# Turning the fourth plain group by blocks on VectorE, with two changes of the weave, in an attention + Fourier-mix + MLP kernel

## Chip, cores, metric

One core of one Trainium2 chip. The metric is the device time of one execution in microseconds, as the median of several runs. A profile's own span is some 1.8 us shorter than the time of its run.

## The reference

Linear attention with decay over blocks, for batch 4, 8 heads, 768 positions, head size 64; then a Fourier mix of the 4 x 768 x 512 result, a layer norm, and an MLP with 2048 hidden units. All in float32.

```python
# attention, per block of 64 positions
intra = einsum('bhic,bhjc->bhij', qb, kb) * Dmask
out   = einsum('bhij,bhjd->bhid', intra, vb) + einsum('bhid,bhde->bhie', qb * lam_pow, kv_state)
kv_state = lam_block * kv_state + einsum('bhsd,bhse->bhde', kb * rev_pow, vb)
# mix and MLP on x = (4, 768, 512)
u  = x + real(fft(fft(x, axis=1), axis=2))
un = (u - mean(u)) / sqrt(var(u) + 1e-06)
y  = u + maximum(un @ w_ch1, 0) @ w_ch2          # 512 -> 2048 -> 512
```

## The kernel before: the parts that matter

A **front** is one batch's attention and Fourier mix. The mixed rows form 12 groups of 256 rows (4 batches x 3). The first four groups in order are **plain**: their MLP products are woven into the fronts of the later batches, so that TensorE has something to do while a front waits. The other eight are done at the end by a scheme with combined weights (the **late** stage). An MLP product needs the normalised rows transposed. Plain groups are turned on TensorE; late ones by 32x32 blocks on VectorE, and four DMAs per tile put the blocks in place in DRAM:

```python
plain = (b, g) in PLAIN                      # PLAIN = the first four of (b, g)
if plain:
    ut = uts[b, g] = new(up, [128, KO, G * 128], "ut")            # 3 buffers
else:
    to = utd[b, g] = dram.tile([128, KO, G * 128], F32, ...)
for i in range(G):
    un = new(np_, [128, DM], "un", bufs=1)
    # ... two tensor_scalar per tile: (x - mean) * rsqrt
    if plain:
        pt = psum_a([128, KO, 128])                               # a whole PSUM bank
        for c in range(KO):
            mm = nc.tensor.transpose(pt[:, c, :], un[:, 128 * c:128 * c + 128], ident)
            # ... (cut)
        nc.scalar.copy(ut[:, :, 128 * i:128 * i + 128], pt)
    else:
        uq = new(ep, [128, DM], "e")                              # ep has 2 buffers
        nc.vector.transpose(uq, un)
        for r in range(0, 128, 32):
            # ... (cut: dst, src)
            nc.sync.dma_start(dst, src)
    yield 0.7
```

The same two `e` buffers serve the unpacking of the float64 weights, which goes on until 227 us:

```python
e = ep.tile([128, 2 * WP], U16, tag="e", ...)
nc.sync.dma_start(raw, src.bitcast(U32))
nc.scalar.activation(sg, top.bitcast(I16), AF.Sign)               # L216, writes e
# ... L217 to L225: VectorE and ScalarE make one float32 piece of w from raw and e
```

and the loads of each attention chunk are issued by SyncE, like the block stores and the weight loads:

```python
for t, src in ((kt, k), (qt, q), (vt, v)):
    nc.sync.dma_start(t, src[b, :, rows, :].rearrange("h p d -> p h d"))
```

Every `yield` of a generator says how much nominal work it has just handed out; a weave takes plain work by the side of front work in a fixed ratio. The program's order is then rearranged once, when the kernel is built, by a scheduler that knows buffers and estimated times. In the traces here each engine works off its list in the order so fixed.

## Time and profile before

| | before |
|---|---|
| time, median of the first 3 runs (and of 6) | 823.18 us (822.48 us) |
| first plain product; first late product | 96.2 us; 428.1 us |
| TensorE idle, 96.2 to 428.3 us | 6.5 us |
| TensorE busy, share of the span | 97% |
| VectorE, ScalarE busy | 53%, 23% |

The stage to look at lies between the first plain and the first late product. TensorE is the bound there, so what counts is its idle time in that stage and what each piece of it waited for. In the profile lines PE is TensorE, PEld its weight loads, DVE VectorE, ACT ScalarE, POOL GpSimd and SPq SyncE's DMA issues; L332 is line 332 of the kernel; `sc<-pa` means that `sc` is written from `pa`, and `A <- B` that A waited for B.

### The profile page before, as it was taken

How to read it: one execution, taken by the hardware profiler on the slowest of the kernel's cores; microseconds unless marked ns; L12 is line 12 of the kernel's file. 1: busy time of each engine (PE TensorE's matmuls, PEld its weight loads, DVE VectorE, ACT ScalarE, POOL GpSimd, SP SyncE). 2: the span in 40 equal slices, each digit the busy share in tenths (PEclk: the TensorE clock that was granted, in tenths of full speed). 3: DMA queues.
4: the chain of work that ended last, by engine and by line, in shares of the span. 5: the costliest groups of instructions: out<-in, count | busy, mean ns of one | idle time of the engine just before them, and what ended most of it. 6: DMA issues, size and time to landing. Idle time of an engine off the chain costs nothing.

```text
span 819.4 us, 11694 instructions
## 1 busy us (share of the span) xinstructions
PE 795.2 (97%) x4608; PEld 634.9 (77%) x4608; DVE 437.8 (53%) x1018; ACT 186.5 (23%) x448; POOL 86.1 (11%) x102
## 2 busy tenths in 40 slices
PE   6989899999999999999999999999999999999998
PEld 5777767768585857768648888888888888888886
DVE  5899798766743761354895541165313661146311
ACT  3756344225420211312002200022001210022100
POOL 3223340011011010220000000000000000000000
PEclk9999999999999999999999999999999999999999
DMA  9979624248741136530351011100111001010010
GB/s 233 249 154 271 174 90 129 63 113 201 203 125 51 52 62 131 129 123 26 93 162 42 1 53 51 52 1 1 64 40 52 0 1 39 33 33 0 1 39 26
DMA packets 126684, 68.88 MB, mean 84 GB/s; under 512 B 111150, under 2 KB 112174, under 8 KB 126630
## 3 DMA queue, kind: packets, MB, share of 16 engines
q1 hardware_dynamic: 121488, 55.67, 26.6%
q0 software_dynamic: 2112, 6.69, 2.4%
q10 hardware_dynamic: 3030, 5.78, 1.9%
q8 instruction: 36, 0.59, 0.3%
q14 instruction: 18, 0.15, 0.1%
HBM read 48.72 MB, written 19.40 MB: 83 GB/s over the span
## 4 chain that ended last, share of the span: by engine, by line
PE 80%; DVE 10%; issue 4%; DMA 3%; ACT 2%; POOL 1%; POOLq 0%; ACTq 0%; DVEq 0%
PE p L770 24%; PE p L723 24%; PE pm L650 10%; PE pm L636 8%; PE pa L332 3%; PE pa L516 3%; PE pa L298 3%; DMA x<-xb,ix 2%; PE pa L328 2%; PE pa L274 1%; DVE sc L302 1%; PE pa L315 1%; PE pa L348 1%; PE pa L279 1%; DVE stt L546 1%
## 5 line engine op out<-in xcount | busy, mean ns | idle before, releaser
L636 PE MATMUL pm<-ut,w 128*128 128x256 f32 x512 | 119.2, 382 | 0.0
L650 PE MATMUL pm<-w,hr 128*128 128x512 f32 x256 | 115.8, 597 | 0.2 <-DVE w L225 0.2
L636 PEld LDWEIGHTS pm<-ut,w 128*128 128x128 f32 x512 | 94.4, 190 | 15.4 <-issue 3.6
L723 PE MATMUL p<-ur,w 128*128 128x256 f32 x384 | 93.8, 379 | 0.0
L650 PEld LDWEIGHTS pm<-w,hr 128*128 128x128 f32 x256 | 46.6, 190 | 49.5 <-issue 48.0
L723 PEld LDWEIGHTS p<-ur,w 128*128 128x128 f32 x384 | 73.0, 190 | 10.3 <-issue 0.5
L723 PE MATMUL p<-us,w1s 128*128 128x256 f32 x256 | 65.7, 379 | 0.0
L770 PE MATMUL p<-w,hs 128*128 128x256 f32 x256 | 58.0, 379 | 0.5 <-DVE y L791 0.5
L770 PE MATMUL p<-w2s,hs 128*128 128x256 f32 x256 | 57.9, 379 | 0.0
L770 PE MATMUL p<-w,ha 128*128 128x256 f32 x256 | 57.9, 379 | 0.0
L770 PEld LDWEIGHTS p<-w,hs 128*128 128x128 f32 x256 | 48.5, 190 | 7.5 <-DVE y L791 0.9
L625 POOL DMA_INDIRECT out_dram<-y,ix x12 | 11.9, 989 | 402.6 <-DVE y L796 342.6
L770 PEld LDWEIGHTS p<-w2s,hs 128*128 128x128 f32 x256 | 48.6, 190 | 6.6
L723 PEld LDWEIGHTS p<-us,w1s 128*128 128x128 f32 x256 | 48.6, 190 | 6.6
L770 PEld LDWEIGHTS p<-w,ha 128*128 128x128 f32 x256 | 48.6, 190 | 6.6
L750 ACT COPY ha<-p 128x256 f32<-128x256 f32 x32 | 11.9, 372 | 169.1 <-PE p L723 139.4
L761 DVE TENSOR_TENSOR ha<-p,ha 128x256 f32<-128x256 f32 x32 | 13.6, 424 | 45.2 <-ACT ha L760 45.2
L298 PEld LDWEIGHTS pa<-qT,kT 64*128 64x128 f32 x384 | 26.0, 193 | 13.2 <-ACT qT L281 7.3
L302 DVE TENSOR_TENSOR sc<-pa,decay 128x512 f32<-128x512 f32 x48 | 31.5, 683 | 8.8 <-PE pa L298 8.5
L332 PE MATMUL pa<-sc,v 128*64 128x128 f32 x384 | 32.1, 284 | 4.1 <-DVE sc L302 4.1
L298 PE MATMUL pa<-qT,kT 64*128 64x128 f32 x384 | 30.7, 292 | 3.2 <-ACT qT L281 2.9
L270 POOL TENSOR_TENSOR kd<-k,decay 128x512 f32<-128x512 f32 x20 | 23.0, 1152 | 94.8 <-PE pa L315 64.5
(144 smaller groups left out, 1135.0 us busy)
## 6 DMA issues: line engine op xcount, KB each, us to landing
raw<-in_moe_w_ch_dram SPq DMA_DIRECT2D x32, 512.0 KB, 4.8
k<-in_k_dram SPq DMA_DIRECT2D x24, 256.0 KB, 5.0
q<-in_q_dram SPq DMA_DIRECT2D x24, 256.0 KB, 5.9
v<-in_v_dram SPq DMA_DIRECT2D x24, 256.0 KB, 4.9
ud<-x SPq DMA_DIRECT2D x16, 256.0 KB, 2.3
utd<-e SPq DMA_DIRECT2D x64, 64.0 KB, 2.2
u<-ud SPq DMA_DIRECT2D x16, 256.0 KB, 2.7
ur<-utd SPq DMA_DIRECT2D x6, 512.0 KB, 4.3
```

The lines of the kernel that those rows point to most:

```text
L270: nc.gpsimd.tensor_tensor(kd, kt, kpow, op=ALU.mult)
L298: mm(pss[hi][:, hp, :], lhsT=kT[HD[hi], hp, :], rhs=qT[HD[hi], hp, :], start=True, stop=True)
L302: nc.vector.tensor_tensor(t, pss[hi], decay[:, hi::2, :], op=ALU.mult)
L328: mm(po[HD[hi], hp, :], lhsT=s_old[HD[hi], hp, :], rhs=qs[HD[hi], hp, :], start=(hp == 0), stop=False, skip_group_check=True)
L332: mm(po[HD[hi], hp, :], lhsT=vt[:, 2 * hp + hi, :], rhs=sc[hi][:, hp, :], start=(c == 0 and hp == 0), stop=(hp == HP - 1), skip_group_chec ...
L516: mm = nc.tensor.matmul(ps[0:m, n, :], lhsT=piece(a, i, n), rhs=cs[0:rows, a, i in (2, 3), n, :], start=(a == 0), stop=(a == 1))
L625: nc.gpsimd.indirect_dma_start(out=out.rearrange("b s d -> (b s) d"), out_offset=row_of(2 + HC * (b + 1) + T - HC), in_=y[:, :], in_offset ...
L636: nc.tensor.matmul(ps, lhsT=w1[:, c, 128 * fc:128 * fc + 128], rhs=ut[:, c, :], start=(c == 0), stop=(c == KO - 1))
L650: nc.tensor.matmul(ps, lhsT=hr[(fc - f0) // 4][:, fc % 4, 128 * i:128 * i + 128], rhs=w2[:, fc, :], start=(fc == f0), stop=(fc == f1 - 1))
L723: nc.tensor.matmul(ps, lhsT=s2.A[a][:, kt, 128 * i:128 * i + 128], rhs=U[b][:, kt, :], start=(first and kt == 0), stop=(kt == 1), skip_gro ...
L761: V.tensor_tensor(a22, two(Z), a22, op=ADD)
L770: nc.tensor.matmul(ps, lhsT=h[a][:, s, i, :], rhs=s2.B[b][:, i, :], start=(first and i == 0), stop=(i == HF - 1), skip_group_check=True)
```

## The change

The intent: take eight transposes, with the wait ahead of them and two parked PSUM banks, off TensorE for the fourth plain group by turning it on VectorE; put more plain work where the last batch's first chunk waits for its masked scores; and keep some more plain work for the handover to the late stage.

```diff
-        yield 1.5
+        yield 3.0 if (b, c) == (B - 1, 0) else 1.5
...
-                    mm(pu[HD[hi], hp, :], lhsT=kd[:, h, :], rhs=vt[:, h, :], start=True, stop=True)
+                    i = mm(pu[HD[hi], hp, :], lhsT=kd[:, h, :], rhs=vt[:, h, :], start=True, stop=True)
+                    if (b, c, h) == (B - 1, 0, 0):
+                        tc.keep_in_program_order(i)
...
-            plain = (b, g) in PLAIN
-            if plain:
+            plain, turned = (b, g) in PLAIN, (b, g) in PLAIN[:3]
+            if turned:
...
+    def fetch(n):
+        ut = uts[PLAIN[n]] = new(up, [128, KO, G * 128], "ut")
+        nc.sync.dma_start(ut, utd[PLAIN[n]])
...
+        if f0 > 0 and (b, g) == PLAIN[1]:
+            fetch(3)
...
-    t_rest, t_back = 3 * t_front - 5 * t_chunk, len(PLAIN) * t_mlp - 50.0
+    t_rest, t_back = 3 * t_front - 5 * t_chunk, len(PLAIN) * t_mlp - 54.0
```

(The second `if plain:` became `if turned:` too.)

More of the change, by code (lines that the diff above doesn't have):

```diff
@@ L565, in norm @@
                                             op0=ALU.subtract, op1=ALU.mult)
-                if plain:
+                if turned:
                     pt = psum_a([128, KO, 128])
```

## The prediction

> **What bounds the kernel now.** I read the stretches first: one table with busy times for the loading stage (0 to 96 us), the mixed stage in which fronts (attention and Fourier mix) and plain products (the MLP of four groups, lines L636 and L650) share TensorE (96 to 404), the handover (404 to 428.5) and the late stage of combined products.
>
> ```profile
> core 0: us, PE busy (x) PEld busy (x) DVE busy (x) ACT busy (x) POOL busy (x), PEclk, DMA share, GB/s
> 0.00:96.00 96.00, 82.31 (x930) 67.15 (x931) 80.73 (x167) 53.03 (x117) 30.47 (x38) 1.00 0.87 215
> 96.00:404.00 308.00, 301.54 (x1832) 216.97 (x1831) 189.73 (x432) 85.42 (x204) 46.86 (x55) 1.00 0.42 110
> 404.00:428.50 24.50, 24.50 (x59) 10.98 (x58) 24.41 (x30) 0.00 (x0) 0.02 (x1) 1.00 0.45 116
> 428.50:819.40 390.90, 386.84 (x1792) 339.84 (x1790) 142.88 (x391) 48.06 (x128) 8.76 (x9) 1.00 0.09 29
> ```
>
> TensorE is the bound from 96 us on, at full clock. In the mixed stage it is idle for 308.00 - 301.54 = 6.46 us; in the handover it is never idle, but VectorE is full too (24.41 of 24.50). The change is not in force before 96 us, and the late stage's work is untouched. So time can come only from those 6.46 us, or from TensorE work that goes away. The list of TensorE's waits in 96 to 428 says whose they are (total, times, longest):
>
> ```profile
> PE pa L569 <- DVE un L564: 2.6, 3, 1.0
> PE pa L516 <- DVE fe L475: 2.1, 3, 1.0
> PE pa L332 <- DVE sc L302: 1.6, 1, 1.6
> PE pm L650 <- DVE w L225: 0.2, 1, 0.2
> ```
>
> They add up to 6.5, so nothing is missing. L569 is the TensorE transpose of a normalised plain group; three of the four groups show a wait there in this stretch. L332 waits once, for the masked scores `sc`. The timeline of TensorE places both. First the turning of the fourth plain group, batch 1 group 1 (columns: start, duration, what, count, idle before and its releaser):
>
> ```profile
> 147.63 0.76 PE L569 MATMUL pa<-ident,un 128*128 128x128 f32 x4 [0.94 <-DVE un L564]
> 148.23 1.03 PE L636 MATMUL pm<-ut,w 128*128 128x256 f32 x4
> 149.10 0.60 PE L569 MATMUL pa<-ident,un 128*128 128x128 f32 x4
> 149.54 0.39 PE L529 MATMUL pa<-dt,ys 128*128 128x128 f32 x2
> ```
>
> then the last batch's first chunk:
>
> ```profile
> 290.70 1.45 PE L650 MATMUL pm<-w,hr 128*128 128x512 f32 x3
> 292.08 0.69 PE L315 MATMUL pa<-v,kd 128*64 128x64 f32 x16
> 294.35 0.43 PE L332 MATMUL pa<-sc,v 128*64 128x128 f32 x2 [1.59 <-DVE sc L302]
> ```
>
> Last, ScalarE's copies out of PSUM. The transposes of the fourth group end near 149.7, but its two copies run here, as one row of the timeline:
>
> ```profile
> 245.83 1.07 ACT L573 COPY ut<-pa 128x512 f32<-128x512 f32 x2 [1.34 <-PE pm L636]
> ```
>
> The `ut` pool has three buffers and this is the fourth group, so the copies wait until the first group's second half has read its buffer. Meanwhile two of the five `pa` banks of PSUM are held for about 245.8 - 149.7 = 96 us.
>
> **What the Trainium skill says.** "TensorE: Matmul & The Clock Gate", Part 4: PE-mode transpose: a full 128x128 transpose in one shot, but the output goes to PSUM and has to be copied out. The trace agrees: eight L569 matmuls and two 0.53 us copies for this group. "VectorE: DVE Perf Modes", The three transpose paths: VectorE turns 32x32 blocks only, not the whole tile. The trace agrees: each block-turned tile (L577, 128x512) is followed by four DMAs that put the blocks in place; one L577 takes 682 to 712 ns (median 700). "PSUM — Partial Sum Buffer", The four PSUM rules: a matmul output is at most one bank, 512 fp32 columns. `pt` is 512 columns, a whole bank, so the two parked tiles are two of the 5 + 3 banks that the pools hold.
>
> **Part 1, the fourth group turned by blocks.** Removed from TensorE: eight transposes. First four: the next matmul starts at 148.23, so 148.23 - 147.63 = 0.60 us of slot (they run in two bursts as the halves of `un` arrive). Second four: 149.54 - 149.10 = 0.44 us. Also the 0.94 us idle ahead of the first. L636 products follow these transposes at once and their `ut` is older, so I take it that TensorE goes on with them. Sum 0.60 + 0.44 + 0.94 = 1.98 us, all on the path, because TensorE is the bound at that point. Removed from ScalarE: two copies, 1.07 us, and an in-order wait of 1.34 us; ScalarE is busy 85 of 308 us here, so worth nothing by itself. Two `pa` banks come free, but no TensorE wait between 150 and 245 is in the list, so I count 0 for them.
>
> Added: two L577 of 0.70 us on VectorE at 148 to 150. There it waited anyway (0.53 us before the second `un` pair, 2.21 us before the L599 at 151.38), so 0 on the path. Added to the DMA queue of SyncE: eight 64 KB stores (median 2.2 us to landing) and one 512 KB fetch (the same transfer by `ur<-utd` took 4.3 us). The fetch can run once the first `ut` buffer is free, near 246 us. The group's first product comes about 362 (L636 has no instances between 326 and 362, where group three ends and four begins). Over 100 us of slack: 0 on the path.
>
> **Part 2, more plain products in the last batch's first chunk.** After the masked scores the front hands back 3.0 units in place of 1.5. The weave ratio is about 0.85, so 1.5 more units call for some 1.3 more units of plain work. This is granular: here the next item is an L650 step of four column blocks, 8 matmuls, and a run of 8 takes 3.4 to 3.6 us in the chain of waits. The pin keeps the state product L315 behind them. The stall is 1.59 us, so one step covers it: -1.6 us. It is the same product, done earlier, not more work.
>
> **Part 3, 54 units kept in place of 50.** The step of 3.4 units taken earlier would be missing at the handover, where VectorE's chain (combining weights, L700, then L713 to L716) ends at 427.88 + 0.68 = 428.56 us, and TensorE's plain products end at 428.3. There is no slack: had TensorE got there 3.6 us sooner with the fronts' end unmoved, it would wait. Four units more held back than before, less the 3.4 spent, bring the fronts' end forward by 0.6 us on top of what parts 1 and 2 save, so VectorE's chain ends earlier by about 3.6 + 0.6 = 4.2 us and TensorE's by 3.6. Own worth: 0, but it lets the other two arrive.
>
> **Sum.** -1.98 - 1.59 = -3.6 us; 823.18 - 3.6 = 819.6 us, ratio 0.9957.
>
> **Rivals.** (a) VectorE becomes the bound at the handover. For it: the last stretch is 24.41 of 24.50 us full on VectorE and both engines end within 0.3 us of each other. Against it: part 3, whose size matches. If it bites, 2 to 3.6 us come back: 821.5 to 823. (b) The interleaving shifts and makes other waits. Two L516 waits of about 1 us (258.9 to 260.0 and before 372.37) hang on VectorE's folding `fe` coming just too late; freed banks let batch 2's front run closer to its place, and the new weave ratio moves plain work around both. Either can vanish or double: -2 to +2 us. For it: all waits in the list are VectorE results arriving about 1 us late. Against it: the order of work within the fronts is unchanged. (c) The block path costs in the queue: the two turned tiles take both `e` buffers, which unpacking of weights (L216 at 151.22) also uses, until the stores land about 4 us later. In the list a late weight cost TensorE only 0.2 us, and the last weight is ready at 227 us, some 20 us before the products of the second half that read it; up to +1 us. (d) The fetch blocks the queue behind it: its landing slot falls where SyncE issues little (only `v` at 240.02 and `out_dram` at 253.48 between 234 and 254), so under 0.5 us. (e) Freed banks help more than I count, by fewer changes between attention and plain products: up to -1.5 us.
>
> **Range and chances.** The middle is -3.6. Rivals (a), (c) and (d) pull up, (b) is even, (e) pulls down. Runs of the kernel before spread over 821.59 to 825.39, so a median can be off by 1 us by itself. I take 819.6 with 816.8 to 822.8 for 8 in 10. Faster by over 2% would need 16.5 us, more than the whole idle time of the mixed stage: 1%. Slower by over 2% would need a new stall of 20 us net: 1%.
>
> **What would show it.** Right: L569 has 24 matmuls and not 32, L573 6 copies and not 8, L577 18 and not 16, 72 stores to `utd` and not 64; the wait of L569 falls from 2.6 to about 1.7 us; the 1.6 us of L332 is gone; TensorE's idle time between 96 us and the first late product falls from 6.5 to about 4, and the late stage starts near 424.7 us and lasts 391 us as before. Wrong: a new wait on `us` or `w1s` at the start of the late stage (rival a), larger waits on `fe` at L516 (b), TensorE waiting on `w` (c), L332 still waiting on `sc` (part 2's step did not come to lie there), or a time before 96 us that has moved, which nothing here explains.

## The result

826.95 us (825.71 to 828.04, 6 runs) against 822.48 us: ratio 1.0050, 95% interval 1.0031 to 1.0069. The change made the kernel slower by 0.5% where 0.4% faster was predicted; the time lies outside the predicted range. A ratio here is the mean time of one kernel's runs over that of the other's of the same rounds, so not quite the ratio of the medians quoted.

In the changed kernel the lines below the edits have moved: L332 is now L335, L516 L519, L569 L572, L577 L580, L581 L584, L636 L645, L644 L653, L650 L659.

The engines' instructions come in the same order in both kernels up to some 135 us, and the late stage lasts 391.3 and 391.2 us. The first plain product was at 96.2 and 97.1 us: that difference comes before the orders part, so it belongs to the two executions and not to the change (in the profiles of all runs it lies between 95.4 and 99.2 us). From the first plain to the first late product it took 331.9 us before and 335.7 us after. The loss lies there. Stretches of that stage, kernel before (columns: stretch, its length, then busy time and instructions of TensorE, weight loads, VectorE, ScalarE, GpSimd, clock, DMA share, GB/s):

```profile
96.20:155.00 58.80, 56.00 (x265) 41.69 (x264) 49.12 (x119) 22.94 (x56) 11.41 (x9) 1.00 0.33 107
155.00:210.00 55.00, 55.00 (x360) 37.02 (x359) 40.05 (x82) 21.59 (x45) 7.14 (x10) 1.00 0.65 162
```

and the changed kernel (one stretch more; before, it was 194.00 long with 190.34 us busy):

```profile
97.05:155.00 57.95, 56.03 (x265) 41.55 (x264) 50.04 (x122) 22.15 (x57) 11.66 (x9) 1.00 0.34 99
155.00:210.00 55.00, 48.66 (x343) 33.81 (x342) 36.79 (x77) 20.93 (x42) 7.54 (x10) 1.00 0.66 164
210.00:404.00 194.00, 189.93 (x1204) 137.22 (x1203) 102.10 (x234) 40.79 (x103) 27.59 (x34) 1.00 0.40 102
```

Length less TensorE's busy time is its idle time. In the first stretch it fell from 2.80 to 1.92 us: the wait ahead of the fourth group's transposes is gone, as predicted. In the second it rose **from 0 to 6.34 us**. This is where the time went, 10 to 45 us after the group was turned. The list of TensorE's waits in the changed kernel (96 to 433 us; total, times, longest) has three lines there that the list of before does not have:

```profile
PE pa L519 <- DVE fe L478: 2.8, 4, 1.0
PE pa L274 <- DMA k<-in_k_dram: 2.6, 1, 2.6
PE pm L645 <- ACT hr L653: 2.1, 1, 2.1
PE pa L572 <- DVE un L567: 1.7, 2, 1.0
PE pa L298 <- ACT qT L281: 1.5, 1, 1.5
PE pa L335 <- DVE sc L302: 1.4, 2, 1.3
PE pm L659 <- DVE w L225: 0.2, 1, 0.2
```

TensorE waits for a load (`k`), for a relu copy out of PSUM (`hr`) and for a copy (`qT`): 2.6 + 2.1 + 1.5 = 6.2 us. None of the three tiles belongs to the fourth group. Its own wait fell as forecast (L569's 2.6 us to L572's 1.7 us), and the wait for `sc` shrank by 0.2 us only.

**The late k load.** The timeline of SyncE's issues, kernel before (start, time from the first start to the last end of the merged issues, what, count):

```profile
172.44 5.27 SPq L581 DMA_DIRECT2D utd<-e  x8
...
181.24 0.38 SPq L263 DMA_DIRECT2D k<-in_k_dram  x1
```

and the changed kernel:

```profile
172.12 0.42 SPq L209 DMA_DIRECT2D raw<-in_moe_w_ch_dram  x1
182.36 5.70 SPq L584 DMA_DIRECT2D utd<-e  x8
...
189.29 0.38 SPq L263 DMA_DIRECT2D k<-in_k_dram  x1
```

In both, the k load of batch 2's third chunk stands behind the eight block stores of batch 1's last group. Those stores went out from 172.4 us before and from 182.4 us after; nothing at all is issued between 172.5 and 182.4. So the k load went out 8.05 us later. The next line is from TensorE's timeline of the changed kernel:

```profile
195.50 0.63 PE L274 MATMUL pa<-ident,k 128*128 128x128 f32 x4 [2.57 <-DMA k<-in_k_dram]
```

Why were the stores late? Batch 1 now has three block-turned groups, six tiles, in place of two groups. They pass through the two `e` buffers, alternately with the weight unpacking. The order in which VectorE does all this was fixed when the kernel was built. VectorE's timeline of the changed kernel:

```profile
173.70 0.69 DVE L285 TENSOR_TENSOR qs<-pa,qpow 128x512 f32<-128x512 f32 x1 [5.37 <-ACT qT L281]
...
180.96 0.42 DVE L217 TENSOR_SCALAR e<-raw 128x512 uint16<-128x512 uint16 x1
...
181.63 0.70 DVE L580 STREAM_TRANSPOSE e<-un 128x512 f32<-128x512 f32 x1
```

The last group's first block transpose (L580) stands behind a chunk of attention and a piece of weight unpacking (L217), and while its turn has not come VectorE idles 5.37 us for `qT`.

**The late relu copies.** ScalarE's timeline of the changed kernel:

```profile
182.59 0.58 ACT L338 COPY oT<-pa 128x512 f32<-128x512 f32 x1 [0.46 <-PE pa L335]
186.75 0.66 ACT L216 ACTIVATE e<-raw 128x512 bf16<-128x512 int16 x1 [3.57 <-DMA utd<-e]
...
187.92 0.91 ACT L653 ACTIVATE hr<-pm 128x256 f32<-128x256 f32 x3
```

The weight unpacking L216 needs an `e` buffer and waits 3.57 us for the landing of a block store that still reads it. Three relu copies stand behind it in ScalarE's order, so three product banks of PSUM stay full and TensorE waits 2.1 us. The `qT` wait at 161.5 us comes through the same list, though no buffer is waited for there: the copies of kT and qT stand behind an L218 that had waited 3.92 us for VectorE's L217, and L217 stood behind norm work in VectorE's order.

**The sc wait.** The extra plain step came where it should: eight L659 matmuls from 293.5 us, between the state product and L335. But VectorE does the two halves of the masked scores apart:

```profile
295.68 0.65 DVE L302 TENSOR_TENSOR sc<-pa,decay 128x512 f32<-128x512 f32 x1
296.25 0.69 DVE L580 STREAM_TRANSPOSE e<-un 128x512 f32<-128x512 f32 x1
...
298.17 0.65 DVE L302 TENSOR_TENSOR sc<-pa,decay 128x512 f32<-128x512 f32 x1
```

In the kernel before they follow each other (two L302 in 1.28 us from 293.62). Now 1.9 us of batch 2's block transpose and norm (L580, L549, L567, L550) come between, so the step covers the wait for the first half and TensorE waits 1.27 us for the second. The 1.59 us of before were for the first half alone: L332 began at 294.35, right after it, and the second was ready when TensorE came to it.

### The profile page after: what moved, and what is told of

Same layout as the page of the kernel before. It is cut to its first block, busy times and chain, and to the rows that moved or that the text cites. A ratio compares the mean times of both kernels' runs of the same rounds, so it can differ in the third digit from the quotient of the medians.

```text
span 823.9 us, 11693 instructions
## 1 busy us (share of the span) xinstructions
PE 792.8 (96%) x4600; PEld 633.3 (77%) x4600; DVE 437.2 (53%) x1020; ACT 184.9 (22%) x446; POOL 86.7 (11%) x102
## 4 chain that ended last, share of the span: by engine, by line
PE 77%; DVE 12%; DMA 4%; issue 4%; ACT 2%; POOL 1%; SPq 0%; DVEq 0%; POOLq 0%; ACTq 0%
PE p L779 24%; PE p L732 23%; PE pm L659 9%; PE pm L645 7%; PE pa L335 3%; PE pa L519 3%; PE pa L298 2%; DMA x<-xb,ix 2%; PE pa L331 1%; DMA raw<-in_moe_w_ch_dram 1%; DVE sc L302 1%; PE pa L316 1%; DVE w L224 1%; PE pa L274 1%; DVE stt L549 1%
## 5 line engine op out<-in xcount | busy, mean ns | idle before, releaser
L645 PE MATMUL pm<-ut,w 128*128 128x256 f32 x512 | 119.2, 382 | 2.1 <-ACT hr L653 2.1
L659 PE MATMUL pm<-w,hr 128*128 128x512 f32 x256 | 115.2, 596 | 0.2 <-DVE w L225 0.2
L645 PEld LDWEIGHTS pm<-ut,w 128*128 128x128 f32 x512 | 94.3, 190 | 17.4 <-issue 3.1
L659 PEld LDWEIGHTS pm<-w,hr 128*128 128x128 f32 x256 | 46.9, 190 | 50.9 <-issue 49.6
L628 POOL DMA_INDIRECT out_dram<-y,ix x12 | 11.8, 987 | 406.9 <-DVE y L805 344.1
L302 DVE TENSOR_TENSOR sc<-pa,decay 128x512 f32<-128x512 f32 x48 | 31.2, 681 | 9.5 <-PE pa L298 9.4
L298 PEld LDWEIGHTS pa<-qT,kT 64*128 64x128 f32 x384 | 25.2, 193 | 14.1 <-ACT qT L281 7.7
L335 PE MATMUL pa<-sc,v 128*64 128x128 f32 x384 | 31.9, 284 | 3.4 <-DVE sc L302 3.3
L298 PE MATMUL pa<-qT,kT 64*128 64x128 f32 x384 | 29.9, 291 | 4.6 <-ACT qT L281 4.3
```

The lines of the kernel that those rows point to most:

```text
L298: mm(pss[hi][:, hp, :], lhsT=kT[HD[hi], hp, :], rhs=qT[HD[hi], hp, :], start=True, stop=True)
L302: nc.vector.tensor_tensor(t, pss[hi], decay[:, hi::2, :], op=ALU.mult)
L335: mm(po[HD[hi], hp, :], lhsT=vt[:, 2 * hp + hi, :], rhs=sc[hi][:, hp, :], start=(c == 0 and hp == 0), stop=(hp == HP - 1), skip_group_chec ...
L628: nc.gpsimd.indirect_dma_start(out=out.rearrange("b s d -> (b s) d"), out_offset=row_of(2 + HC * (b + 1) + T - HC), in_=y[:, :], in_offset ...
L645: nc.tensor.matmul(ps, lhsT=w1[:, c, 128 * fc:128 * fc + 128], rhs=ut[:, c, :], start=(c == 0), stop=(c == KO - 1))
L659: nc.tensor.matmul(ps, lhsT=hr[(fc - f0) // 4][:, fc % 4, 128 * i:128 * i + 128], rhs=w2[:, fc, :], start=(fc == f0), stop=(fc == f1 - 1))
```

## The experiments

Theory A: the six block-turned tiles of batch 1 contend with the weight unpacking for `e`, and their stores hold up the loads behind them in SyncE's list. Rival B: the new weave ratio moves the work. Rival C: more 128-byte packets make all transfers slower. "Waits" below are TensorE's from the waits list, for qT, hr and k.

| run | time us | ratio to before [95%] | waits qT, hr, k (us) |
|---|---|---|---|
| changed kernel | 826.95 | 1.0050 [1.0031, 1.0069] | 1.5, 2.1, 2.6 |
| e1 turning alone | 824.06 | 1.0025 [1.0009, 1.0040] | 0.5, 0.8, 2.4 |
| e2 scheduling parts alone | 820.72 | 0.9984 [0.9965, 1.0004] | none |
| e3 54 kept alone | 821.29 | 0.9986 [0.9970, 1.0002] | none |
| e4 chunk part alone | 821.81 | 1.0006 [0.9984, 1.0029] | none |
| e5 changed, half of the tiles staged in y | 826.51 | 1.0046 [1.0028, 1.0064] | none, none, 4.0 |
| e6 changed, one chunk's loads on ScalarE's queue | 822.23 | 0.9994 [0.9980, 1.0009] | 1.5, 1.0, 0.6 |
| e7 both | 822.80 | 1.0008 [0.9992, 1.0024] | none, 1.0, 1.3 |
| e8 before, half of the tiles in y | 821.55 | 0.9984 [0.9970, 0.9998] | none |
| e9 changed, all tiles in y | **818.67** | **0.9947 [0.9927, 0.9967]** | none |
| e10 before, one chunk's loads on ScalarE's queue | 820.74 | 0.9993 [0.9969, 1.0016] | none |
| e11 changed, two chunks' loads on ScalarE's queue | 819.75 | 0.9968 [0.9950, 0.9986] | 1.8, none, none |
| e12 changed, last group's stores on ScalarE's queue | 828.66 | 1.0073 [1.0051, 1.0095] | 1.5, 4.3, none |
| e13 before, all tiles in y | 822.84 | 1.0003 [0.9984, 1.0023] | none |
| e14 turning alone, all tiles in y | 820.12 | 0.9976 [0.9957, 0.9995] | none |
| e15 scheduling parts alone, all tiles in y | 821.17 | 0.9978 [0.9964, 0.9992] | none |

Kernels are compared only within the same rounds. All outputs were correct.

**The granted clock differs between these runs, too.** The record gives each run's mean granted TensorE clock: 0.999 on average for the runs of the kernel before, 0.998 for the changed kernel, 0.994 for e12. By these means the clock can account for about 1 us of the changed kernel's 4.5 us (an estimate: 0.1% of 825 us), though not for the loss in its profiled execution, which has full clock over the whole stage. In the traces, which list the clock from the first 11 to 14 us on, it is full up to the last microseconds but for ten stretches at 0.5, nine of 3.4 us and one of 6.8 us. One such stretch costs up to 1.7 us (an estimate: half of 3.4). Each begins during or within 1.8 us after an idle time of TensorE of 1.2 us or more; in e1 it begins at 192.8 us, after the k wait that ends at 191.9. Most idle times of that length are followed by none, and whether the idle time brings the stretch on is not shown. Five of the ten lie in the stage looked at here: in e1, e3, e5, e12 and e14.

### One part at a time: e1 to e4

e1 is the changed kernel with `yield 1.5`, no pin and `- 50.0`:

```diff
-        yield 3.0 if (b, c) == (B - 1, 0) else 1.5
+        yield 1.5
-                    if (b, c, h) == (B - 1, 0, 0):
-                        tc.keep_in_program_order(i)
-    ... len(PLAIN) * t_mlp - 54.0
+    ... len(PLAIN) * t_mlp - 50.0
```

> The change without its two scheduling parts: the fourth plain group is turned by blocks and fetched, the last batch's first chunk hands back 1.5 units and 50 units are kept, as before. Theory A (six block-turned tiles of batch 1 share two small staging buffers with the weight unpacking, and their stores stand in the load queue ahead of the next chunk's k load): the stalls of the changed kernel at 160 to 203 us come back here (qT about 1.5 us, hr about 2.1, k load about 2.6), while the 0.94 us wait of the fourth group's transposes and 0.9 us of transposes are gone; the last batch's sc wait of 1.6 us stays. Time 823 + 7.0 - 2.0 = 826 to 829 us. Rival B (the new weave ratio of 54 kept units moves the work of 150 to 200 us): no such stalls, 820 to 822 us. Rival C (eight more stores of 128-byte packets make all DMA slower): slower too, 825 to 829, but with k and raw loads longer from issue to landing and issued no later than before.

Measured 824.06 us: slower, though below the range given. The same three waits are there, together 3.7 us and not 6.2. So the turning by itself brings them, and rival B falls as an account of them. (The profile also has a stretch at half clock, from 192.8 us, so not all of e1's loss need be these waits.)

e2 is the changed kernel with `turned = (b, g) in PLAIN` and no fetch; e3 has of the scheduling parts only `- 54.0`, e4 only the 3.0 units and the pin.

> The change without the turning: 3.0 units and the pin in the last batch's first chunk, 54 units kept; the fourth group stays on TensorE. Theory A: no stalls of over 1 us between 150 and 203 us other than the 1.1 us ahead of the fourth group's transposes; time within 2 us of before: 821 to 825 us. Rival B: the stalls of the changed kernel at 160 to 203 us are here: 826 to 829 us. In either case it shows whether the 1.6 us wait for sc goes away without the turning.

> Only 54 units kept in place of 50. Theory A: 822 to 824 us, no new stall over 1 us before 200 us; the sc wait of about 1.6 us in the last batch's first chunk stays. Rival B: 826 to 829 us with the stalls at 160 to 203 us.

> Only the 3.0 units and the pin in the last batch's first chunk, 50 kept. If one more plain step in that place covers the wait for sc, L332's wait falls from 1.6 us to below 0.3 us and the time to 821 to 822 us. If the wait only moves to the second sc tile, as in the changed kernel (1.27 us), the time stays within 1 us of before: 822 to 824 us. Less plain work is then left for the handover: up to 2 us may come back there as a wait for us.

None of the three has a wait for qT, hr or k. Times of 820.7 to 821.8 us, with intervals that include 1, or nearly end there. e4's wait for `sc` is still 1.6 us, e2's 1.3 us and e3's 0.9 us. But **e4 is no test of the filler step**: it did not come to lie there. Between L298 and L335 TensorE has the same six plain matmuls, all ahead of the state product, as in the kernel before, and the wait is again for the first half. The step is in place in e2, as in the changed kernel, and wins 0.3 us; e3, which lacks the edit but has some plain matmuls there by its new ratio, wins 0.7 us, against its expectation. So what is won of the wait for `sc` depends on where the halves of `sc` come to lie, and not on the filler step alone. What makes e2 some 0.2% faster, if anything, is not in its waits (its wait for `fe` even grew from 2.1 to 3.3 us); that stays open.

By sum, turning (+0.25%) and scheduling (-0.16%) would give +0.1%; together they gave +0.5%. Of that difference, some 3.4 us, the growth of the three waits from 3.7 to 6.2 us is 2.5 us; the intervals are wide enough to hold the rest.

### What the waits hang on: e5 to e8

e5 stages the first tile of each of batch 1's groups in `y`, a buffer of the same size that lies unused until 250 us. (A further buffer of its own does not fit: the build has 0.34 kB per partition left.)

```diff
-                    uq = new(ep, [128, DM], "e")
+                    uq = new(up, [128, DM], "y", bufs=1) if b == 1 and i == 0 else new(ep, [128, DM], "e")
```

> The changed kernel, with the first block-turned tile of each of batch 1's three groups staged in the y buffer, which nothing uses before 250 us, so that the two e buffers are not asked for six tiles. Theory A1 (the staging buffers are the cause): the third group's block transposes run near 172 us and not at 182 to 185, its stores and the k load behind them go out before 182 us, and the waits of 2.1 us for hr and 2.6 us for k are gone or below 0.5 us each; time 827 - 5 = 821 to 823 us. Rival A2 (only the place of the k load in the queue matters): the hr wait stays. Rival C (more small packets slow all transfers): no gain over the changed kernel, 826 to 828 us.

The waits for hr and qT are gone, as A1 expects, but the k wait is 4.0 us and a wait for `sc` near 167 us came besides. The waits listed sum to 11.0 us, against 12.3 in the changed kernel, but a stretch at half clock follows the k wait, and in time nothing is gained. SyncE's timeline of e5 says why the k load is still late:

```profile
169.75 2.66 SPq L584 DMA_DIRECT2D utd<-y  x4
183.12 2.59 SPq L584 DMA_DIRECT2D utd<-e  x4
...
188.45 0.38 SPq L263 DMA_DIRECT2D k<-in_k_dram  x1
```

The last group's first tile, in y, goes out at 170 us, its second, in e, only at 183, and the k load stands behind that one. So A1 as stated, that half of the tiles would do, was wrong.

e6 leaves the buffers and issues three loads elsewhere:

```diff
-            nc.sync.dma_start(t, src[b, :, rows, :].rearrange("h p d -> p h d"))
+            (nc.scalar if (b, c) == (2, 2) else nc.sync).dma_start(t, src[b, :, rows, :].rearrange("h p d -> p h d"))
```

> The changed kernel, with the k, q and v loads of batch 2's third chunk issued from ScalarE's queue in place of SyncE's, ahead of the block stores and no longer behind them; staging buffers as in the changed kernel. Theory A1: the 2.6 us wait for k is gone, the 2.1 us wait for hr and the 1.5 us wait for qT stay: 827 - 2.6 = 823.5 to 825 us. Rival A2 (the queue alone): all waits at 180 to 203 us go, 821 to 823 us. Rival C: no gain.

822.23 us: better than the 823.5 to 825 expected from the k wait alone. ScalarE's queue issued k at 159.63 us; the stores still went out from 181.76 us, as in the changed kernel. The k wait of the third chunk is gone (0.6 us is left for the fourth's) and the hr wait has halved; the qT wait is untouched at 1.5 us. The time lies in the range given for A2, but not all waits went, so neither reading fits whole. What e5 and e6 show together: **the qT wait goes with the staging and not with the place of the loads; the k wait goes with the place of its load; the hr wait is reduced by either.**

> Both edits together, on the changed kernel. If the two act on the same stall (theory A1), the time is that of the staging edit alone within 1 us: 820 to 823 us. If they act on different ones it is lower by 2 us or more than either.

e7, both edits, is no better than e6: the fourth chunk's k and q loads (1.3 and 0.9 us of waiting) are now the late ones, and an hr wait of 1.0 us is back. Neither reading of the expectation fits (822.80 lies in its first range, but the staging edit alone took 826.51): each edit rearranges the whole list, and the edits do not add.

> Control: the kernel before, with the first block-turned tile of each of batch 1's two block-turned groups staged in y. It had no wait over 0.1 us there, so nothing to win: 821 to 824 us under every theory. A gain of over 2 us here would say that the edit helps for another reason than the change.

e8, the control: 821.55 us, within what was expected, with no new or lost wait over 0.5 us.

### The full staging edit, its controls, and the other queue: e9 to e12

```diff
-                    uq = new(ep, [128, DM], "e")
+                    uq = new(up, [128, DM], "y", bufs=1) if b == 1 else new(ep, [128, DM], "e")
```

> The changed kernel, with all six block-turned tiles of batch 1 staged in the single y buffer, none in the e buffers. e5 had left the second tile of the third group in e, and it still ran at 183 us with the k load of batch 2's third chunk behind its stores (wait 4.0 us). If what matters is only that this k load goes out late, the time follows the k load here: its place in SyncE's queue is ahead of the last two tiles' stores, so the k wait falls below 1 us and the time to 821 to 824 us. If the e buffers themselves matter, the hr and qT waits are gone too and it is 820 to 822 us. One buffer for six tiles can itself make waits (each tile's stores take some 4 us to land), up to 2 us more.

818.67 us, faster than expected, and faster than both kernels. TensorE's list of waits from 97 us to the handover of e9:

```profile
PE pa L519 <- DVE fe L478: 2.6, 4, 1.0
PE pa L572 <- DVE un L567: 1.7, 2, 1.0
PE pa L335 <- DVE sc L302: 1.3, 1, 1.3
```

and SyncE's timeline, for comparison with the two above:

```profile
169.67 0.56 SPq L209 DMA_DIRECT2D raw<-in_moe_w_ch_dram  x1
170.34 0.39 SPq L263 DMA_DIRECT2D k<-in_k_dram  x1
177.53 2.60 SPq L584 DMA_DIRECT2D utd<-y  x4
```

The block stores are not earlier than before, they are later still (the sixth tile's go out from 193.95 us), since one buffer takes one tile at a time. But the loads now stand between them, k at 170.34 us, and the unpacking has both `e` buffers to itself. All three waits are gone. This also rules out rival C, that the number of packets is what costs: e9 issues the same stores and the same fetch as the changed kernel. On the pages, the median k load took 5.0 us from issue to landing before, 5.8 us in the changed kernel and 5.5 us in e9, a small thing beside an issue that is 8 us late. What e9 does not separate is the wait for an `e` buffer from the order: the order is fixed by a scheduler that knows the buffers, so the staging edit changes both.

> Control for e6: the kernel before, with the k, q and v loads of batch 2's third chunk issued from ScalarE's queue. Before had no wait for k there, so if the queue's order is the cause of the loss in the changed kernel there is nothing to win: 821.5 to 823.5 us. A gain of 2 us or more would say that e6's gain has another reason.

e10: ratio 0.9993, nothing gained, as expected of a kernel that has no such wait (its median, 820.74 us, lies 0.8 us under the range given).

e11 is e6 with `b == 2 and c in (2, 3)`:

> As e6, with the loads of batch 2's fourth chunk on ScalarE's queue too. e6 was left with 0.6 us of waiting for the fourth chunk's k and 1.0 us for hr at 189 us, at 822.2 us. If the queue is the cause of both, 820.5 to 821.5 us; if the hr wait comes from ScalarE's own order (it stands behind a weight unpacking that waits for an e buffer), it stays and the time is 821.3 to 822.3 us.

819.75 us, better than the range for either reading: the waits for hr and k are both gone and the qT waits (1.8 us) are left. So the place of the loads alone can remove the hr wait, although the blocks still pass through `e`.

e12 moves the last group's block stores, not the loads:

```diff
-                        nc.sync.dma_start(dst, src)
+                        (nc.scalar if (b, g) == (1, 0) else nc.sync).dma_start(dst, src)
```

> The changed kernel from the other side: the loads stay on SyncE's queue and the eight block stores of the third group (batch 1, group 0) go to ScalarE's. Queue theory: k and raw loads go out ahead of 176 us, the k wait is gone, the time 821 to 824 us. ScalarE pays for it: eight issues of about 0.6 us in its order, where an hr copy stands behind them, so an hr wait of up to 3 us may stay.

828.66 us, the slowest of all; the estimate of 821 to 824 was wrong, and so was the 3 us given as the most for hr. The k wait is gone, but ScalarE's timeline of e12 shows what took its place:

```profile
183.55 7.53 ACTq L584 DMA_DIRECT2D utd<-e  x8
191.18 0.65 ACT L216 ACTIVATE e<-raw 128x512 bf16<-128x512 int16 x1 [7.05 <-DMA k<-in_k_dram]
...
192.35 0.64 ACT L653 ACTIVATE hr<-pm 128x256 f32<-128x256 f32 x2
```

The eight stores take 7.53 us of ScalarE's order, waits for VectorE's transposes included, and the relu copies stand behind them: 4.3 us of waiting for hr. (The releaser named in L216's line, the k load, is the last event the profile saw; what stands ahead of L216 in ScalarE's order are the stores.) The blocked stores hurt in either list. That e12 is slower than the changed kernel is not in its waits, which sum to 11.8 us in the stage against 12.3, but goes with the clock: its profile is at half clock for 6.8 us from 190.6 us, inside and after the hr wait.

### Whose gain is it: e13 to e15

> The kernel before, with all four block-turned tiles of batch 1 staged in y. If e9's gain is the change's own, before gains nothing from the edit: 821.5 to 823.5 us, and the 1.1 us ahead of the fourth group's transposes stays. If the edit is what gains, 818 to 820 us.

> e1 (the turning alone) with all of batch 1's block-turned tiles staged in y. The prediction's first step put the turning at -2.0 us; without the stalls at 155 to 203 us that should now show: 820 to 821.5 us, with the 1.75 us stall for sc in the last batch's first chunk still there. If it is 818 to 819.5 us the scheduling parts add nothing.

> e2 (the scheduling parts alone, fourth group on TensorE) with y staging. As e2: 820 to 822 us, since e2 had no stall at 155 to 203 us to take away. If it reaches 819 us or less, e9's gain owes nothing to the turning.

The staging edit gives the kernel before nothing (e13, 1.0003). The turning with it is worth -0.24%, or 2.0 us of 822 (e14), which agrees with the prediction; the interval reaches from 0.4 to 3.5 us. (In e14's profile the stage is 0.7 us shorter than before, with a half-clock stretch of up to 1.7 us in it.) The scheduling parts are worth -0.2% (e15); e15 has a wait list like e2's. Both together -0.53% (e9), about the sum. e14 also shows rival (a) of the prediction in small: with 50 units kept, TensorE waits 0.2 us at the first late products, which e9, with 54, does not. e9, of which there are four runs, is the version to keep: the intervals of its ratio and of the changed kernel's do not overlap. Those of e11, e14 and e15 do overlap with it, so that it beats these is not shown.

## Why the prediction was wrong

**Counts and places, right.** 24 L572 matmuls, 6 copies into `ut`, 18 block transposes and 72 stores are in the profile after. The fetch was issued at 250 us with over 100 us of slack. The late stage did not change. Some readings of the prediction were off without bearing on the sum: the two copies took 0.58 to 0.59 us each and overlap, so 1.07 us is not twice 0.53; L636 begins again at 360.5 us, not 362; the first of the two L516 waits ends at 260.45 us.

**Part 1, removed: right as far as the runs resolve it.** -1.98 us predicted. The wait of 0.9 us is gone from the list in every run that turns the group by blocks, and e14, without the side effects, measures -0.24%.

**Part 1, added, "0 on the path": this is the step that failed.** The prediction priced each added instruction by its own duration and its own deadline: two transposes into idle VectorE time, eight stores of 2.2 us, a fetch with slack. What it did not price is what stands behind them in the lists that run in order, and that the scheduler would order these lists anew. Rival (c) had the mechanism, "the two turned tiles take both e buffers", and looked for its cost in the wrong place: in late weights, with "up to +1 us". The weights were indeed hardly late for TensorE (0.2 us, as before). The relu copies behind the unpacking were (2.1 us), and qT (1.5 us), and the k load behind the stores (2.6 us). Rival (d) looked at the fetch, which did no harm, and not at the stores. The term put at 0, with +1 us as the worst case, measured 6.2 us in the changed kernel and 3.7 us with the turning alone (e1). It also came from the wrong group: the fourth group's own stores went out at once, at 150.5 us; the group that turned last in batch 1 paid, 32 us later.

**Part 2, "one step covers it: -1.6 us": wrong in mechanism.** The step did come to lie there. But the prediction took the wait to be one wait with a fixed end, at 294.35 us. That was the end of the first half of `sc` only; VectorE's order is rearranged together with TensorE's, and the second half slipped behind norm work. 0.3 us was won, in e2 as in the changed kernel; in e4 the step did not come to lie there.

**Part 3: worth about nothing alone, as said** (e3, interval up to 1.0002), and right about the danger, which e14 shows at 0.2 us.

**The sum.** Predicted -3.6. Measured in the profiles from first plain to first late product: +3.75 us. TensorE's idle time there went from 6.5 to 1.92 + 6.34 + 4.07 = 12.3 us, +5.9, and the transposes' slots took 1.0 us away; that leaves about -1.1 us, which no wait explains. TensorE changes between attention and plain products 120 times in this stage in place of 128 (counted in the traces), which is rival (e)'s kind; whether that is the cause was not tested. In e9 the same stage takes 328.5 us, against 331.9 less 3.6 = 328.3 predicted: the size came out about right for a kernel without the contention, but in part by luck: the 1.6 us of part 2 did not come (0.3 us did), TensorE's idle time is only 0.7 us less than before and the slots 1.0 us, so about half of the gain has no cause shown.

## What to carry to other kernels

A step moved off the bounding engine can be paid for in every in-order list that it enters, and the bill may come to an unrelated instruction far behind it; ask of each added DMA and buffer use what stands next in that list and who takes the buffer next, not only whether it has slack itself. When a move that should win loses, look for waits that are new on tiles the change never touched, then free the shared buffer and reorder the queue in separate runs: here each removed some of the three waits and moved others, since every edit also rearranged the lists, and a buffer that was idle at that time turned +0.5% into -0.5%. Before comparing times of a fraction of a percent, look at the granted clock of the runs as well as at their waits. Filling a wait with other work helped little here, because the engine that ends the wait did not keep its own order.

## What the Trainium skill lacked or had wrong

- "DMA: Bandwidth & Descriptors", Issuing engines are not separate DMA queues, says that issuing from several engines "will only save the time on the sequencer it takes to initiate the DMA, which is usually small relative to the DMA itself". Here the time saved was not the issue time but a wait: on SyncE the k load stood behind block stores whose data came 10 us late (no issue from 172.5 to 182.4 us); issued by ScalarE it went out at 159.63 us, in 0.39 us, and the kernel went from ratio 1.0050 to 0.9994 (e6). A DMA that waits for its data held up every later DMA of the same issuer. The page does say, in "Anatomy of one DMA" (which follows GpSimd's path), that a DMA's semaphore wait (for the signal that its data is there) happens on the issuing sequencer; what the section lacks is this consequence. Nor does the section say what issuing costs a compute engine: eight stores took 7.53 us of ScalarE's order, waits included, and the copies behind them made TensorE wait 4.3 us (e12).
- "VectorE: DVE Perf Modes", The three transpose paths, compares the paths by the duration of the transpose. Where only blocks are turned, it leaves out the copies that put them in place, which cost more here: one block transpose of 128x512 took 0.70 us, the four stores of a tile took some 2.6 us of SyncE's issue time, and the staging buffer is held until they land (an issue to landing of 2.2 us).
